# Rank 20 products for one block of units or for two at once, in a retention block with a maxout FFN

## The chip, the cores and the metric

The kernel runs on one core of one Trainium2 chip. The metric is the device time of a run in microseconds (us), the median over several runs. The profile is one further execution of the same program, recorded instruction by instruction.

The engines appear under their short names in the profile: PE is TensorE (matmuls; PEld are its weight loads), DVE is VectorE, ACT is ScalarE, POOL is GpSimd, SP is the engine that issues most of the transfers. TensorE writes its sums to PSUM[...].

## The reference

The first half is retention in parallel form, over 8 batches, 8 heads, 576 positions, head size 64; the second is a feed-forward network with a maximum of three products:

```
scores = scale * q @ k.T
ret    = scores * Dmat            # gamma_h ** (i - j) for i >= j, else 0
x      = (ret @ v)  as (B*S, H*D) # 4608 tokens x 512
h      = max(x @ w1, x @ w2, x @ w3)   # 4608 x 768
out    = h @ w_out                # 4608 x 512
```

Everything is fp32 here; the weights come as float64 and are converted on the chip.

## The kernel before, in words

**Tiles and stages.** The tokens are cut into 9 tiles of 512 (`t` = 0 to 8), each of four chunks of 128. While the feed-forward network of tile `t` runs, the retention of tile `t + 1` is woven into it. The last loop does this: `steps(t + 1)` gives twelve lists of retention steps, and after each list the generator `ffn(t)` is advanced by one part. The engines take their instructions in program order, so this loop, together with two lists of small deferred steps, sets the order. `soon` appends VectorE work of the retention to `urgent`; `chore` pops one step from `urgent` (or from `chores`, which holds sums of weights); `scale` pops one multiplication of keys by their decay on ScalarE. Inside the products these pops are made at fixed step numbers (lines 785 to 793).

**Retention.** Chunks 0 to 7 go through transposed keys and queries (`transposes`), masked scores (`scores`, tiles `st`), states (`state`, `keep`) and outputs (`values`). From chunk 8 on it is done in halves of 64 positions: `chunk_scores` writes masked scores into the tiles `m0` and `m1` (the latter holds the transposed queries first) and keeps the running state stacked with the values in `va`; `chunk_values` multiplies the two. VectorE transposes, masks, adds the states and scales the output into `xT`; GpSimd multiplies the state in `va` by the decay `gs_of` (line 335).

**The up products.** `h` of a tile has 6 blocks of 128 units (`fb`), taken in pairs (`fp`). Tile 0, and pair 1 of tile 1, are computed plainly (`up_plain`). All others use a scheme in which 20 products stand for the 24 that a block needs for 512 tokens: each multiplies a combination of weight blocks (`w_sb`, `n`, summed once by `weight_sums`) with a combination of quarters of `x` (`s`, summed per tile by `sums_of_x`), 256 tokens wide. `PRODUCTS` gives their order:

```
PRODUCTS = """E a11 b12, E a14 b42, B s15 n5, A a22 b21, C s3 b23, B s19 b41, A s10 b32, C a13 b31, B s6 n2, A s13 b22,
              C a11 b11, B s14 n1, A s11 n4, D s7 b43, B a23 n6, A s20 b33, D s16 b13, B a21 n3, A a21 n8, A a24 n7"""
```

The letters are five chains of sums in PSUM, which differ in where they end. A and B take turns in the two banks of `ps_x`; E, C and D take turns in the two banks of `ps_y`, so D uses E's bank and the next E uses C's. A product is named by its chain and its number there: A3 is the third on chain A. After most products the running sum of the chain is copied by ScalarE to SBUF into a `part` (line 698), and the chain goes on adding in the same bank. `JOINS` lists what VectorE then adds, or takes the maximum of, to turn parts into the two halves of `h` (line 693): 14 copies and 14 joins per block. Two of the joins read a chain's bank directly: B1's reads E, C3's reads C. The last nine joins of a block follow D2 (three), B6 (three) and A7 (three); B6's first one gives the low half of `h` (tokens 0 to 255), A7's last one gives the high half.

`up` does this for one block `fb`: 20 products, one at a time, with banks half used (256 of 512 values). In tile 1 the blocks come in the order 2, 3, 0, 1, 4, 5, in later tiles 0, 1, 4, 5, 2, 3.

**The down products.** `downs` multiplies `h` with `w_out` by seven products of half-size blocks, in the order 1, 2, 6, 7, 5, 4, 3; each runs over all three pairs `fp` and both halves of 128 tokens, 12 matmul instructions. Product 1 reads the low half of `h` for the even block of every pair, product 2 for the odd block; 6, 7, 5 and 3 read sums of `h` that `sums_of_hidden` makes on VectorE and GpSimd. `kept` copies a product's bank to parts, `total` adds it to another product and stores.

**Buffers.** `ppool` holds the parts, 20 slots of 1 KB under the tag `part`; the decay table `gs` and the states of the first eight chunks are in the same ring. `att` holds `kT` (2 buffers), `m0` and `m1` (3 each).

Of the kernel before, what the change touches and what calls it, by code (L numbers as in the profile page):

```python
# [53 lines left out]
AHEAD = 3  # L54
FILL = 192
PARTS = 20

# [24 lines left out]
def kernel(  # L82
# [184 lines left out]
    def transposes(g):  # L267
        both = qks[g] = {}
        if g >= BY_CHUNKS:
            for n, tag in (("k", "kT"), ("q", "m1")):  # L270
                both[n] = att.tile([P, H, D], FP32, tag=tag, name=tag, bufs=2 if n == "k" else 3)
            ms[g, 0], ms[g, 1] = att.tile([P, H, D], FP32, tag="m0", name="m0"), both["q"]
        else:
            for n in ("k", "q"):
                tag, bufs = ("kT", 2) if n == "k" else (f"m{g % 2}", 3)
                both[n] = att.tile([P, NP, C], FP32, tag=tag, name=n + "T", bufs=bufs)
        if g >= BY_PE:
            for n in ("k", "q"):
                soon(partial(nc.vector.transpose, both[n][:].rearrange("a p c -> a (p c)"),
                             raws.pop(("kx" if n == "k" else n, g))[:].rearrange("a x y i -> a (x y i)")))  # L280
            return
        for n, src in (("k", raws["k", g]), ("q", raws.pop(("q", g)))):
            pool, tag = (ps_r, "r") if g >= CPT else (ps_x, "x")
            pt = pool.tile([P, NP, C], FP32, tag=tag, name=n + "t")
            for p in range(NP):
                nc.tensor.transpose(pt[:, p, :], pair(src, p), ident[:C, :C])
            nc.scalar.copy(both[n][:], pt[:])

    def scores(g):
        chore(len(urgent))  # L290
        scale(len(scaling))
        if g >= BY_CHUNKS:
            chunk_scores(g)
            return
        qT, kT = qks[g]["q"], qks[g]["k"]
        s = [ps_r.tile([C, NP, C], FP32, tag="r", name=f"s{j}") for j in range(2)]
        for p in range(NP):
            for j in range(2):
                r = slice(D * j, D * (j + 1))
                nc.tensor.matmul(s[j][:, p, :], lhsT=kT[r, p, :], rhs=qT[r, p, :], start=True, stop=True)  # L300
        for j in range(2):
            st = sts[g, j] = att.tile([C, NP, C], FP32, tag=f"m{j}", name="st")
            soon(partial(nc.vector.tensor_tensor, st[:], s[j][:],
                         masks[start_of(g)][:].unsqueeze(1).to_broadcast([C, NP, C]), op=ALU.mult))
# [44 lines left out]
    def state_factors():  # L349
        for j in range(2):  # L350
            nc.scalar.copy(gs_of[half(1), j::2].unsqueeze(2), gs[half(j), :, 0:1])

# [15 lines left out]

    def keep(g):
        def step(t, kv):  # L370
            if start_of(g) is not None:
                nc.vector.tensor_tensor(t[:], kv[:], gs[:], op=ALU.mult)
            else:
                nc.vector.tensor_tensor(t[:], kv[:], states[g][:], op=ALU.add)
                nc.gpsimd.tensor_tensor(t[:], t[:], gs[:], op=ALU.mult)
# [156 lines left out]
    def downs(t, h):  # L532
# [4 lines left out]
        def summed(n):  # L537
# [6 lines left out]
              5: summed(1), 6: summed(2), 7: summed(3)}  # L544

        def bank(pool, tag, name):
            b = pool.tile([P, NM, DM // 2], FP32, tag=tag, name=name)
            return [(m, whole, b[:, m, :]) for m in range(NM)]

# [52 lines left out]
        for group in ([[piece] for piece in x] if last else [x]):  # L602
            product(3, group, False)
            for m, cols, o in group:
# [78 lines left out]

    def up(t, h, fb):

        lo, hi = h[:, fb, 0:NH], h[:, fb, NH:NT]
        ps, of = {}, {}  # L690

        def join(out, a, b, op=ALU.add):
            nc.vector.tensor_tensor(out, a, b, op=op)  # L693

        def after(step):
            if step not in ("E1", "E2", "C2", "C3", "A6", "B5"):
                t = of[step] = ppool.tile([P, NH], FP32, tag="part", name="part")
                nc.scalar.copy(t[:], ps[step[0]][:])  # L698
            for out, ins, op in JOINS.get(step, ()):
                ins = [ps[n[0]] if n in ("E", "C") else of[n] for n in ins]  # L700
                join({"lo": lo, "hi": hi}.get(out) if out in ("lo", "hi") else of[out][:],
                     *(x[:] for x in ins), op)

        done = {}
        for chain, x, w in PRODUCTS:
            n = done[chain] = done.get(chain, 0) + 1
            if n == 1:
                pool, tag = (ps_x, "x") if chain in "AB" else (ps_y, "y")
                ps[chain] = pool.tile([P, NH], FP32, tag=tag, name=chain.lower())
# [3 lines left out]
            nc.tensor.matmul(ps[chain][:], lhsT=factor(w, fb), rhs=xS[t][x], start=n == 1, stop=ends,  # L713
                             skip_group_check=True)
            after(f"{chain}{n}")
            yield

# [25 lines left out]
    def ffn(t):  # L743
# [28 lines left out]
        if t == 1:  # L772
            spread.append(True)
            weight_sums(0)
            weight_sums(2)
        plain = (2, 3) if t == 1 else ()
        order = (2, 3, 0, 1, 4, 5) if t == 1 else (0, 1, 4, 5, 2, 3)
        total = sum(24 if fb in plain else len(PRODUCTS) for fb in order)
        count = parts = 0
        for n, fb in enumerate(order):  # L780
            if fb not in plain:
                while fb // 2 not in summed_fp:
                    chore()
            steps_of_one = up_plain_all(t, h, fb) if fb in plain else up(t, h, fb)
            for step, cost in enumerate(steps_of_one):
                if fb in plain:
                    chore(4 if (fb, step) == (plain[-1], 1) else 8)
                elif step % 4 == 1 or step % 4 == 3 and len(urgent) > 6:
# [9 lines left out]
            if n % 2:  # L798
                sums_of_hidden(h, fb // 2)
                if fb in plain:  # L800
                    weight_sums(fb // 2)
        chore(len(urgent))
# [6 lines left out]

    def up_plain_all(t, h, fb):  # L810
        for i in range(3):
            up_plain(t, h, fb, i)()
            yield 8
# [146 lines left out]
```

## Time and profile before

| | |
|---|---|
| time, median of three runs | 764.6 us (763.73 to 766.52) |
| the profiled run | 763.31 us, span of its trace 761.3 us |
| TensorE busy | 749.7 us (98%), 5928 matmul instructions |
| VectorE busy | 594.4 us (78%) |
| ScalarE busy | 385.6 us (51%) |
| GpSimd busy | 91.5 us (12%) |
| joins (line 693), part to part | 460 at a mean of 470 ns |
| copies of chains (line 698) a and b | 276 at 369 ns, 230 at 372 ns |
| granted TensorE clock | full throughout |

A row of instruction groups in the profile reads: line, engine, operation, names of what is written and read, shape, count, then busy time and the mean of one in ns, then the idle time of the engine just before these instructions and which instruction ended most of it. In a row of waits the engine, name and line before the arrow waited for the one behind it; then follow the total in us, the number of times and the longest. In the timeline each row is a start, a length, an engine and an instruction, with the number merged into the row.

One fp32 matmul of the program is two matmul instructions on TensorE, so 920 products appear as 1840.

### The profile page before, as it was taken

What the parts mean: (1) busy time and instruction counts of PE and PEld (TensorE: products, weight loads), DVE (VectorE), ACT (ScalarE), POOL (GpSimd) and SP (SyncE); (2) the same over time, 40 slices, a digit from 0 to 9 for tenths busy, and PEclk for the clock granted to TensorE, in tenths of its full rate; (3) what the DMA queues carried; (4) which work ended last, traced back from release to release, by engine and by line L of the source; (5) the groups of instructions that cost most, each with busy time, mean ns of one, the idle gap of its engine ahead of it and who ended that gap; (6) DMA issues with size and microseconds to landing.
All of it is one profiled execution on the core that took longest, in us unless ns stands there. A gap on an engine that the chain in (4) does not pass through costs nothing.

```text
span 761.3 us, 16127 instructions
## 1 busy us (share of the span) xinstructions
PE 749.7 (98%) x5928; PEld 604.7 (79%) x5928; DVE 594.4 (78%) x1274; ACT 385.6 (51%) x1051; POOL 91.5 (12%) x112
## 2 busy tenths in 40 slices
PE   8999999999999999999999999999999999999998
PEld 7645444688878888888888888888888888888887
DVE  2998998979888967797788859885889677955771
ACT  3664641365256635664466446643665266515551
POOL 3210122102010111011011102010102011100000
PEclk9999999999999999999999999999999999999999
DMA  9995753404241514242333324242414141000001
GB/s 222 242 240 130 200 108 80 87 9 84 80 81 34 91 45 96 45 74 54 81 74 58 68 69 87 37 79 65 90 29 94 45 91 33 2 29 28 1 1 56
DMA packets 230318, 59.39 MB, mean 78 GB/s; under 512 B 211168, under 2 KB 228960, under 8 KB 230240
## 3 DMA queue, kind: packets, MB, share of 16 engines
q1 hardware_dynamic: 229664, 58.04, 35.2%
q8 instruction: 46, 0.75, 0.4%
q10 hardware_dynamic: 576, 0.33, 0.1%
q14 instruction: 32, 0.26, 0.1%
HBM read 48.89 MB, written 9.44 MB: 77 GB/s over the span
## 4 chain that ended last, share of the span: by engine, by line
PE 86%; DVE 9%; SPq 2%; DMA 1%; issue 1%; ACT 0%; DVEq 0%; ACTq 0%
PE a L713 15%; PE b L713 13%; PE dx L553 11%; PE up L736 11%; PE c L713 6%; PE dz L553 5%; PE d L713 5%; PE e L713 4%; DVE part L693 4%; PE o L436 4%; PE down L723 3%; PE dy L553 3%; DVE m L325 2%; PE sk L317 2%; SPq L218 1%; DMA qraw<-in_q_dram 1%
## 5 line engine op out<-in xcount | busy, mean ns | idle before, releaser
L693 DVE TENSOR_TENSOR part<-part 128x256 f32<-128x256 f32 x460 | 211.7, 470 | 62.4 <-ACT part L698 53.9
L698 ACT COPY part<-a 128x256 f32<-128x256 f32 x276 | 101.8, 369 | 65.8 <-PE a L713 60.3
L698 ACT COPY part<-b 128x256 f32<-128x256 f32 x230 | 85.6, 372 | 94.3 <-PE b L713 88.3
L736 PE MATMUL up<-xT,w 128*128 128x512 f32 (+2 forms) x200 | 84.7, 579 | 1.6 <-DVE w L642 1.6
L713 PE MATMUL a<-s,w 128*128 128x256 f32 x276 | 82.2, 380 | 0.0
L713 PE MATMUL b<-s,n 128*128 128x256 f32 x276 | 82.1, 379 | 0.0
L736 PEld LDWEIGHTS up<-xT,w 128*128 128x128 f32 x200 | 36.8, 190 | 43.6 <-issue 38.4
L186 ACT ACTIVATE kraw<-kraw,gk 128x64 f32<-128x64 f32 x208 | 66.9, 349 | 0.7 <-DMA kraw<-in_k_dram 0.4
L713 PE MATMUL d<-s,w 128*128 128x256 f32 x184 | 56.3, 388 | 2.8 <-DVE part L693 2.6
L335 POOL TENSOR_TENSOR va<-va,gs_of 64x512 f32<-64x512 f32 x24 | 26.9, 1120 | 263.9 <-DVE va L333 157.8
L713 PEld LDWEIGHTS b<-s,n 128*128 128x128 f32 x276 | 52.5, 190 | 7.1
L713 PEld LDWEIGHTS a<-s,w 128*128 128x128 f32 x276 | 51.5, 190 | 8.1 <-ACT part L698 0.2
L713 PE MATMUL b<-xT,n 128*128 128x256 f32 x184 | 56.6, 389 | 0.0
L713 PE MATMUL c<-xT,w 128*128 128x256 f32 x184 | 54.9, 380 | 0.0
L713 PE MATMUL e<-xT,w 128*128 128x256 f32 x184 | 47.3, 380 | 0.7 <-DVE part L693 0.7
L713 PE MATMUL a<-xT,n 128*128 128x256 f32 x184 | 47.2, 379 | 0.0
L325 DVE TENSOR_TENSOR m<-sk,gm 64x512 f32<-64x512 f32 x56 | 38.5, 688 | 8.4 <-PE sk L321 7.2
L553 PE MATMUL dx<-To,H 128*128 128x256 f32 (+1 forms) x204 | 44.9, 371 | 0.0
L693 DVE TENSOR_TENSOR h<-part 128x256 f32<-128x256 f32 x92 | 39.1, 425 | 6.9
L713 PEld LDWEIGHTS d<-s,w 128*128 128x128 f32 x184 | 33.7, 190 | 12.7 <-DVE part L693 8.7
L560 ACT COPY part<-dx 128x256 f32<-128x256 f32 (+1 forms) x34 | 10.5, 362 | 63.4 <-PE dx L553 56.7
L553 PEld LDWEIGHTS dx<-To,H 128*128 128x128 f32 x204 | 36.6, 190 | 4.8
(121 smaller groups left out, 1351.9 us busy)
## 6 DMA issues: line engine op xcount, KB each, us to landing
bits<-in_moe_w_dram SPq DMA_DIRECT2D x36, 256.0 KB, 4.9
out_dram<-osb SPq DMA_DIRECT2D x35, 256.0 KB, 2.1
kraw<-in_k_dram SPq DMA_DIRECT2D x32, 256.0 KB, 3.1
qraw<-in_q_dram SPq DMA_DIRECT2D x224, 32.0 KB, 2.1
kxraw<-in_k_dram SPq DMA_DIRECT2D x224, 32.0 KB, 2.1
va<-in_v_dram SPq DMA_DIRECT2D x56, 128.0 KB, 3.1
bits<-in_moe_w_out_dram SPq DMA_DIRECT2D x6, 512.0 KB, 6.4
vraw<-in_v_dram SPq DMA_DIRECT2D x7, 256.0 KB, 4.6
```

What stands on the lines that cost most here:

```text
L186: scaling.popleft()()
L317: nc.tensor.matmul(sk[c][half(c), h, :], lhsT=kr[half(c), h, :], rhs=vas[g, c][half(c), h, :], start=True, stop=True)
L325: nc.vector.tensor_tensor(ms[g, c][half(c)], sk[1 - c][half(c)], gm[half(c)], op=ALU.mult)
L335: nc.gpsimd.tensor_tensor(to[half(1)], to[half(1)], gs_of[half(1)].unsqueeze(2).to_broadcast([D, H, D]), op=ALU.mult)
L436: nc.tensor.matmul(o[half(c), n % 2, n // 2, half(m)], lhsT=vas[g, m][:, h, :], rhs=ms[g, m][:, h, :], start=m == 0 and n == 0, stop=True, ...
L553: nc.tensor.matmul(o, lhsT=hS[n](fp)[:, m * P:(m + 1) * P], rhs=late["T"][n][:, fp, cols], start=first and fp == 0 and (m == 0 or last and ...
L560: nc.scalar.copy(both[m][:, cols], o)
L693: nc.vector.tensor_tensor(out, a, b, op=op)
L698: nc.scalar.copy(t[:], ps[step[0]][:])
L713: nc.tensor.matmul(ps[chain][:], lhsT=factor(w, fb), rhs=xS[t][x], start=n == 1, stop=ends, skip_group_check=True)
L723: nc.tensor.matmul(b[:], lhsT=h[:, fb, m * P:(m + 1) * P], rhs=w_sb["out", fb], start=(fb == 0), stop=(fb == NF - 1))
L736: nc.tensor.matmul(ps[:, cols], lhsT=w_sb[i, fb][:, dc * P:(dc + 1) * P], rhs=xT[t][:, dc, cols], start=dc == 0 and cols.start == 0, stop= ...
```

## The change

`up` takes a pair of blocks, `fp`, in place of one block. Each of the 20 products is issued for block `2 * fp` and then for `2 * fp + 1`, into the two halves of one PSUM bank; the flag that starts a bank's sums is set on the first of the two alone. Copies and joins follow the second and are 512 wide. The parts that end up as the two halves of `h`, A1 and A2, are copied into `h` at once and joined there, so a pair takes 12 slots of `ppool` where two blocks took 28. The ring has 11 slots, now of 2 KB.

Around it: `kept`, `total` and the last copy of `downs` treat a bank in one instruction. `gs` becomes a constant of 4 values per partition that is broadcast where it is used, and its load fetches 4 bytes per row and head pair in place of 256. The transposed queries of chunks 0 to 7 move from `m0`/`m1` to the ring of parts. `m0` has two buffers, taken in `chunk_scores` and no longer in `transposes`. The order of the pairs is that of the blocks before, and the steps that pop deferred work keep their numbers, counted over 40 steps of a pair and no longer twice over 20. `FILL`, an unused tile, has 160 bytes for 192.

```diff
-FILL = 192
-PARTS = 20
+FILL = 160
+PARTS = 11
...
-         "B6": [("lo", ("A2", "A3"), ALU.max), ("A5", ("A5", "B4"), ALU.add), ("A5", ("A5", "D1"), ALU.add)],
-         "A7": [("A1", ("A1", "B6"), ALU.add), ("A1", ("A1", "A5"), ALU.max), ("hi", ("A1", "A7"), ALU.max)]}
+         "B6": [("A2", ("A2", "A3"), ALU.max), ("A5", ("A5", "B4"), ALU.add), ("A5", ("A5", "D1"), ALU.add)],
+         "A7": [("A1", ("A1", "B6"), ALU.add), ("A1", ("A1", "A5"), ALU.max), ("A1", ("A1", "A7"), ALU.max)]}
...
+    gs = const.tile([P, NP], FP32, name="gs")
-    gs = ppool.tile([P, NP, D], FP32, tag="part", name="gs")
...
-            ms[g, 0], ms[g, 1] = att.tile([P, H, D], FP32, tag="m0", name="m0"), both["q"]
+            ms[g, 1] = both["q"]
         else:
-            for n in ("k", "q"):
-                tag, bufs = ("kT", 2) if n == "k" else (f"m{g % 2}", 3)
-                both[n] = att.tile([P, NP, C], FP32, tag=tag, name=n + "T", bufs=bufs)
+            both["k"] = att.tile([P, NP, C], FP32, tag="kT", name="kT", bufs=2)
+            both["q"] = ppool.tile([P, NP, C], FP32, tag="part", name="qT")
...
-            st = sts[g, j] = att.tile([C, NP, C], FP32, tag=f"m{j}", name="st")
+            st = sts[g, j] = att.tile([C, NP, C], FP32, tag=f"m{j}", name="st", bufs=2 + j)
...
+        ms[g, 0] = att.tile([P, H, D], FP32, tag="m0", name="m0", bufs=2)
         nc.scalar.copy(ms[g, 0][half(1)], ms[g, 1][half(1)])
...
         def kept(src):
-            both = [ppool.tile([P, NH], FP32, tag="part", name="part") for _ in range(NM)]
-            for m, cols, o in src:
-                nc.scalar.copy(both[m][:, cols], o)
+            both = ppool.tile([P, NM, NH], FP32, tag="part", name="part")
+            for m, cols, o in together(src):
+                nc.scalar.copy(both[:, m, cols], o)
...
-            for m, cols, o in src:
-                nc.vector.tensor_tensor(osb[:, m, cols], o, others[m][:, cols], op=ALU.add)
+            for m, cols, o in together(src):
+                nc.vector.tensor_tensor(osb[:, m, cols], o, others[:, m, cols], op=ALU.add)
...
-    def up(t, h, fb):
+    def up(t, h, fp):
+        two = slice(2 * fp, 2 * fp + 2)
+        ps, of = {}, {"A1": h[:, two, NH:NT], "A2": h[:, two, 0:NH]}
...
             if step not in ("E1", "E2", "C2", "C3", "A6", "B5"):
-                t = of[step] = ppool.tile([P, NH], FP32, tag="part", name="part")
-                nc.scalar.copy(t[:], ps[step[0]][:])
+                if step not in of:
+                    of[step] = ppool.tile([P, 2, NH], FP32, tag="part", name="part")[:]
+                nc.scalar.copy(of[step], ps[step[0]][:])
...
-            nc.tensor.matmul(ps[chain][:], lhsT=factor(w, fb), rhs=xS[t][x], start=n == 1, stop=ends,
-                             skip_group_check=True)
-            after(f"{chain}{n}")
-            yield
+            for e in range(2):
+                nc.tensor.matmul(ps[chain][:, e, :], lhsT=factor(w, 2 * fp + e), rhs=xS[t][x],
+                                 start=n == 1 and e == 0, stop=ends, skip_group_check=True)
+                if e == 1:
+                    after(f"{chain}{n}")
+                yield
...
-                nc.sync.dma_start(gs[half(j)], state_decay[half(j), :, half(j)])
+                nc.sync.dma_start(gs[half(j)].unsqueeze(2), state_decay[half(j), :, D * j:D * j + 1])
```

More of the change, by code (lines that the diff above doesn't have):

```diff
@@ L350, in state_factors @@
         for j in range(2):
-            nc.scalar.copy(gs_of[half(1), j::2].unsqueeze(2), gs[half(j), :, 0:1])
+            nc.scalar.copy(gs_of[half(1), j::2], gs[half(j)])
     def key_masks():
@@ L369, in keep @@
     def keep(g):
+        factor = gs[:].unsqueeze(2).to_broadcast([P, NP, D])
         def step(t, kv):
             if start_of(g) is not None:
-                nc.vector.tensor_tensor(t[:], kv[:], gs[:], op=ALU.mult)
+                nc.vector.tensor_tensor(t[:], kv[:], factor, op=ALU.mult)
             else:
                 nc.vector.tensor_tensor(t[:], kv[:], states[g][:], op=ALU.add)
-                nc.gpsimd.tensor_tensor(t[:], t[:], gs[:], op=ALU.mult)
+                nc.gpsimd.tensor_tensor(t[:], t[:], factor, op=ALU.mult)
         if begins(g):
@@ L544, in downs, with together @@
               5: summed(1), 6: summed(2), 7: summed(3)}
+        banks = {}
         def bank(pool, tag, name):
             b = pool.tile([P, NM, DM // 2], FP32, tag=tag, name=name)
-            return [(m, whole, b[:, m, :]) for m in range(NM)]
+            pieces = [(m, whole, b[:, m, :]) for m in range(NM)]
+            banks[id(pieces)] = [(whole, whole, b[:])]
+            return pieces
+        def together(src):
+            return banks.get(id(src), src)
         def product(n, out, first):
@@ L603, in downs @@
             product(3, group, False)
-            for m, cols, o in group:
+            for m, cols, o in together(group):
                 nc.scalar.copy(osb[:, m, cols], o)
@@ L682, in convert @@
             next(converting, None)
-    def up(t, h, fb):
[L689 to L693, printed above, removed]
+    def up(t, h, fp):
+        two = slice(2 * fp, 2 * fp + 2)
+        ps, of = {}, {"A1": h[:, two, NH:NT], "A2": h[:, two, 0:NH]}
         def after(step):
             if step not in ("E1", "E2", "C2", "C3", "A6", "B5"):
-                t = of[step] = ppool.tile([P, NH], FP32, tag="part", name="part")
[L698 to L702, printed above, removed]
+                if step not in of:
+                    of[step] = ppool.tile([P, 2, NH], FP32, tag="part", name="part")[:]
+                nc.scalar.copy(of[step], ps[step[0]][:])
+            for dst, ins, op in JOINS.get(step, ()):
+                a, b = (ps[n][:] if n in ("E", "C") else of[n] for n in ins)
+                nc.vector.tensor_tensor(of[dst], a, b, op=op)
         done = {}
@@ L708, in up @@
                 pool, tag = (ps_x, "x") if chain in "AB" else (ps_y, "y")
-                ps[chain] = pool.tile([P, NH], FP32, tag=tag, name=chain.lower())
+                ps[chain] = pool.tile([P, 2, NH], FP32, tag=tag, name=chain.lower())
             while x not in made[t]:
@@ L775, in ffn @@
             weight_sums(2)
-        plain = (2, 3) if t == 1 else ()
-        order = (2, 3, 0, 1, 4, 5) if t == 1 else (0, 1, 4, 5, 2, 3)
-        total = sum(24 if fb in plain else len(PRODUCTS) for fb in order)
+        plain = 1 if t == 1 else None
+        order = (1, 0, 2) if t == 1 else (0, 2, 1)
+        total = sum(48 if fp == plain else 2 * len(PRODUCTS) for fp in order)
         count = parts = 0
-        for n, fb in enumerate(order):
-            if fb not in plain:
-                while fb // 2 not in summed_fp:
+        for fp in order:
+            if fp != plain:
+                while fp not in summed_fp:
                     chore()
[L784 to L787, printed above, removed]
+            for step, cost in enumerate(up_plain_all(t, h, fp) if fp == plain else up(t, h, fp)):
+                if fp == plain:
+                    chore(4 if step == 4 else 8)
                 elif step % 4 == 1 or step % 4 == 3 and len(urgent) > 6:
@@ L797, in ffn @@
                     yield
[L798 to L801, printed above, removed]
+            sums_of_hidden(h, fp)
+            if fp == plain:
+                weight_sums(fp)
         chore(len(urgent))
@@ L808, in ffn, with up_plain_all @@
         yield
[L810 to L813, printed above, removed]
+    def up_plain_all(t, h, fp):
+        for fb in (2 * fp, 2 * fp + 1):
+            for i in range(3):
+                up_plain(t, h, fb, i)()
+                yield 8
     warm(6)
```

## The prediction

> **What bounds the kernel now.** I read the page's busy table first, then the chain that ended last, then the waits of the weight loads and matmuls, then the timeline around one such wait, then the groups by shape.
>
> ```profile
> PE 749.7 (98%) x5928; PEld 604.7 (79%) x5928; DVE 594.4 (78%) x1274; ACT 385.6 (51%) x1051; POOL 91.5 (12%) x112
> ...
> PE 86%; DVE 9%; SPq 2%; DMA 1%; issue 1%; ACT 0%; DVEq 0%; ACTq 0%
> ```
>
> TensorE is the bound: 98% busy, 86% of the chain. No other engine is near full, so shorter work on VectorE or ScalarE pays only where TensorE stands still for it. Those places are in the weight-load waits (waiter, released by: us in total, times, longest):
>
> ```profile
> PEld d L713 <- DVE part L693: 8.7, 15, 1.4
> ...
> PEld a L713 <- ACT part L698: 3.0, 13, 0.6
> ...
> PEld e L713 <- DVE part L693: 1.1, 1, 1.1
> ```
>
> One of the fifteen, on TensorE and then on VectorE (start, length, instruction, count, idle before it):
>
> ```profile
> 303.23 0.60 PE L713 MATMUL b<-s,n 128*128 128x256 f32 x2
> 303.66 0.66 PE L713 MATMUL a<-s,n 128*128 128x256 f32 x2
> 304.59 0.70 PE L713 MATMUL d<-s,w 128*128 128x256 f32 x2 [0.27 <-DVE part L693]
> 305.12 0.59 PE L713 MATMUL b<-xT,n 128*128 128x256 f32 x2
> ...
> 303.38 0.69 DVE L325 TENSOR_TENSOR m<-sk,gm 64x512 f32<-64x512 f32 x1
> 304.11 0.42 DVE L693 TENSOR_TENSOR part<-e,part 128x256 f32<-128x256 f32 x1
> ```
>
> A product (two matmul instructions) starts every 0.43 us: 303.23, 303.66, and the next should be 304.09. Chain d needs the bank of chain e, which the join of B1 has to read first. That join belongs to the third product, but VectorE is late and runs it at 304.11, after which d starts at 304.59. Lost: 0.50, and 0.10 more, since the next product follows after 0.53. So the idle figure beside the matmul (0.27) understates it.
>
> All such losses: a weight load normally starts 0.21 ahead of its matmul, so 15 waits of 8.7 in total moved the d matmuls by 8.7 - 15 x 0.21 = 5.5 us, plus 15 x 0.10 = 1.5 for the restart: 7.0. Chain e once, at 227.66 instead of 226.78, plus 0.10: 1.0. Of the thirteen a-waits all but one are the usual lead; the long one cost about 0.4. **At most 8.4 us (1.1% of the span) is there to win in the products.**
>
> [...] The trace has 369 to 372 and 571 to 588[...]. [...]
>
> ```profile
> 216.30 1.23 POOL L335 TENSOR_TENSOR va<-va,gs_of 64x512 f32<-64x512 f32 x1 [24.56 <-DVE va L333]
> ...
> 216.54 2.19 DVE L693 TENSOR_TENSOR part<-part 128x256 f32<-128x256 f32 x3
> ...
> 307.02 1.34 DVE L693 TENSOR_TENSOR part<-part 128x256 f32<-128x256 f32 x3 [0.32 <-ACT part L698]
> ```
>
> Three joins take 2.19 beside GpSimd and 1.34 without it: 0.85 dearer. [...]
>
> **The change, part by part.**
>
> ```profile
> L693 DVE TENSOR_TENSOR part<-part 128x256 f32<-128x256 f32 x460 | 211.7, 470 | 62.4 <-ACT part L698 53.9
> L693 DVE TENSOR_TENSOR h<-part 128x256 f32<-128x256 f32 x92 | 39.1, 425 | 6.9
> ...
> L740 DVE TENSOR_TENSOR h<-h,up 128x512 f32<-128x512 f32 x16 | 10.9, 682 | 2.3 <-PE up L736 2.2
> ...
> L741 ACT COPY h<-up 128x512 f32<-128x512 f32 x8 | 4.6, 571 | 10.7 <-PE up L736 10.7
> ```
>
> *Matmuls.* 46 units become 23 pairs with the same 920 products, weight loads and shapes. Nothing is gained on TensorE itself.
>
> *Joins.* 644 (14 per unit) become 322 of double width. A 512-wide operation takes 682 to 732 ns (w<-mant,expo, both inputs in SBUF, 732). From the x3 line a dependent 256-wide join costs 0.447, 0.03 over a lone 0.42, so I take 0.71 for a dependent 512-wide one. Busy time goes from 289 us (with the e and c joins' 38) to 322 x 0.71 = 229. VectorE gains 60 us, all of it beside TensorE, so none of it counts directly.
>
> *Copies.* 644 x 0.37 become 322 x 0.58: 51 us less on ScalarE, also beside TensorE.
>
> *The d and e waits.* D1 is product 13, counted from 0. Before it, VectorE has the previous unit's nine last joins (9 x 0.45 = 4.0 us) plus attention work, against 13 x 0.43 = 5.6 us. In a pair the nine joins take 9 x 0.71 = 6.4 us against 26 x 0.43 = 11.2 us. Margin 4.8 us instead of 1.6, and at most two attention transposes (0.70 each) are queued ahead of the e join. Those waits go. In a chain, the copy (0.04 + 0.58) lies under four steps of 0.43, 1.73 us, where before 0.37 lay under 0.86. So the a wait goes too: minus 8.4.
>
> *The new wait, at the start of the down products.* Product 1 reads the low half of h for even blocks, product 2 for odd. Before, the even block of the last pair was finished a unit earlier. Now both are finished together, by the first join of B6, behind the three of D2. From the end of D2's slot: 0.16 matmul drain, 0.04 to ScalarE, 0.08 for a key scaling ahead of the copy, 0.58 copy, 0.03 to VectorE, 4 x 0.71 joins, 0.06 to TensorE, 0.10 restart = 3.9 us. TensorE gets there after B6, A6 and A7 for two blocks each (six steps of 0.43) and the two steps that read block pair 0: 8 x 0.43 = 3.45. So it stands 0.45 us in tiles 2 to 8 (order of pairs 0, 2, 1). In tile 1 pair 2 is last and is read two matmuls later: nothing. 7 x 0.45 = **plus 3.1**. Bounds: 0 (shorter joins) to 1.3 per tile (a GpSimd scaling beside the joins adds 0.85).
>
> *Score matmuls of the third pair* need the second chunk's transposes, which stand behind the previous pair's nine joins: ready about 6.8 us after the pair's start, needed at 14 x 0.43 + 1.0 = 7.0. That is thin: 0 to 0.6 a tile, I take 0.07: **plus 0.5**.
>
> *h as destination, eleven 2 KB slots.* A1 and A2 are copied into h 3.5 us or more after the last down product read the old h, so ScalarE doesn't wait. A pair takes twelve slots of eleven: slot twelve and the next pair's first fall on parts last read in A3's and D2's joins. The latter end about 2.5 us before the next B1 copy. Nothing.
>
> *kept, total and the last copy of downs.* 512 wide: each delays its reader by about 0.2 us, hidden behind the 2.59 us of the product between.
>
> *qT in the parts' pool, m0 with two buffers taken at the scores.* The scores of a pair follow the values of the pair before, so two suffice; ScalarE's copy into m0 is queued at the same place as before. *FILL* moves addresses only. Nothing for either.
>
> *gs.* 128 KB in 512 packets becomes 2 KB in 512 packets; SP issues two DMAs as before, ahead of later key and value loads. At the 222 GB/s of the first slice 128 KB is 0.6 us, and the first stage waits on loads; packets of 4 bytes aren't free. 0 to 0.6, taken as **minus 0.3**.
>
> Sum: -8.4 + 3.1 + 0.5 - 0.3 = **-5.1 us** on a span of 761.3. That profiled run took 763.31, below the three timed runs' median of 764.6 (763.73 to 766.52), so I put the change on the median: **759.5 us**, 0.7% faster. About 0.5% (3.8 us) is what a measurement of this kernel can tell from no change.
>
> **Rivals.** *Full gain (0.15):* the joins run nearer 0.68 and the products' start is hardly held; only the -8.4 and -0.3 and some 0.5 remain: 756.4. For it: L740's 682. Against it: a dependent chain of four.
> *Hidden anyway (0.15):* VectorE runs in program order, so the e join stays behind masks and transposes and d still waits as often; the new wait eats the rest: 763 to 765. For it: in the example the 0.69 mask was directly ahead of the e join. Against: the margin above.
> *Slower (0.20):* VectorE at the end of a pair becomes the bound. GpSimd's scaling of va (1.12 us), which I expect to end 0.2 us before D2's joins, falls on them: the new wait is 1.3 us, and in the third pair another such overlap turns the thin score margin into 0.55. 7 x 1.85 = 13, less 8.4 and 0.3: about 769. It decides from 1.2 us per tile on (8.4 / 7). For it: joins of 0.73 at 216.54. Against: in the last tile there is no attention, and the overlap needs both places.
>
> **How the numbers follow.** My forecast has 0.50, of which 0.45 is below 760.8 and 0.05 above. Full gain 0.15 is faster; hidden 0.15 is the same; slower 0.20 splits 0.18 and 0.02. Faster 0.60, same 0.22, slower 0.18. The forecast's own range is 757.5 to 761.5; for 8 in 10 it reaches from the full gain with its unknowns (755.5) into the slower case (768).
>
> **What would show it.** Joins: 322, near 0.70. Weight loads of d waiting on a join: gone, from 8.7 us to under 1. A new wait of dx on the h join, seven times, 0.3 to 0.7 us each. Score matmuls waiting on a transpose: under 1 us in all. TensorE's count unchanged. Wrong if dx waits over 1.2 us per tile, if d waits persist, or if the first 25 us stretch.

## The result and the profile after

The changed kernel takes 757.27 us (median of 4 runs, 757.02 to 758.12), the kernel before 764.16 us beside it (4 runs, 763.57 to 766.52): ratio 0.9906, 95% interval 0.9883 to 0.9929. Faster by 0.9%, and 2.2 us below the forecast of 759.5: just below its own range (757.5 to 761.5) and inside that for 8 in 10 (755.5 to 768). The profiled run took 757.02 us, its span is 755.2 us against 761.3 before.

First the busy table of the page after, and the engines' shares of its chain:

```profile
PE 747.1 (99%) x5928; PEld 608.1 (81%) x5928; DVE 535.6 (71%) x929; ACT 342.6 (45%) x700; POOL 91.3 (12%) x112
...
PE 92%; DVE 4%; DMA 2%; ACT 2%; SPq 1%; issue 0%; POOL 0%; DVEq 0%; ACTq 0%; POOLq 0%
```

The 5928 matmuls stay. VectorE lost 58.8 us of work and ScalarE 43.0, in 345 and 351 fewer instructions. None of that appears in the time by itself: VectorE's share of the chain fell from 9% to 4% because TensorE waits for it less. The waits of the weight loads on VectorE or ScalarE that concern the change (waiter, released by: us in total, times, longest):

```profile
PEld dx L562 <- DVE h L708: 3.5, 7, 0.5
...
PEld sk L321 <- DVE m L191: 1.1, 1, 1.1
...
PEld d L720 <- ACT part L705: 0.4, 1, 0.4
```

The fifteen waits of chain d on a join (8.7 us) and that of chain e (1.1) are gone. New are seven of the first down product, `dx`, on the join that completes the low half of `h`, as forecast, one of score matmuls on a transpose, in tile 1, and one of chain d on a copy just behind it. The groups by shape (line, engine, operation, count, busy, mean ns, idle before):

```profile
L708 DVE TENSOR_TENSOR part<-part 128x512 f32<-128x512 f32 x161 | 111.3, 691 | 94.2 <-ACT part L705 91.8
L708 DVE TENSOR_TENSOR h<-h,part 128x512 f32<-128x512 f32 x115 | 79.7, 693 | 28.2 <-ACT h L705 24.2
...
L705 ACT COPY part<-b 128x512 f32<-128x512 f32 x115 | 67.4, 586 | 140.4 <-PE b L720 140.4
```

A join of 512 takes 0.69 us (0.71 forecast) and a copy 0.586 (0.58, from copies of 512 at 571 to 588 ns in the trace before). Both engines now mostly wait for TensorE, or for each other, as their idle columns say: of the 94.2 us of idle time before the joins of parts, 91.8 ended with a copy, and the copies of `b` waited 140.4 us for TensorE.

The new wait, in the timeline at the end of a tile (start, length, instruction, count, idle before it):

```profile
341.14 1.04 POOL L335 TENSOR_TENSOR va<-va,gs_of 64x512 f32<-64x512 f32 x1 [4.74 <-PE a L720]
...
342.33 2.14 DVE L708 TENSOR_TENSOR part<-part 128x512 f32<-128x512 f32 x3 [1.32 <-ACT part L705]
...
344.10 3.15 PE L562 MATMUL dx<-w_out,h 128*128 128x256 f32 x12
344.51 0.69 DVE L708 TENSOR_TENSOR h<-h,part 128x512 f32<-128x512 f32 x1
...
345.25 1.59 PEld L562 LDWEIGHTS dx<-w_out,h 128*128 128x128 f32 x8 [0.53 <-DVE h L708]
```

After its first four `dx` matmuls TensorE needs the pair just finished. Its weight load stands until the `h` join ends at 345.20, behind the three joins of D2. The twelve take 3.15 us where twelve that do not wait take 2.75 (the forecast had 0.45 a tile; this is 0.40). GpSimd's scaling of `va` ended at 342.18, 0.15 us before D2's joins.

Where the time went, from the starts of the first `dx` matmul of each tile in the two timelines. The third row is the later run e1, in which no `dx` waits: a floor for this program.

| us | to the first `dx` of tile 1 | from each to the next, tiles 1 to 8 | sum of the seven |
|---|---|---|---|
| before | 185.56 | 81.72, 79.90, 79.62, 79.75, 80.23, 80.50, 72.34 | 554.06 |
| after | 186.11 | 78.80, 79.19, 79.19, 79.22, 79.19, 79.19, 72.54 | 547.32 |
| e1 | 186.22 | 78.80, 78.80, 78.79, 78.79, 78.80, 78.80, 72.15 | 544.93 |

Before stood 9.1 us above the floor between these marks, after 2.4. That is 6.7 us gained; up to the first mark 0.55 was lost. From the last mark to the end of the span both take 21.7 us. Tile 8's `dx` wait of 0.4 is in the second, but from the start of the last matmul to the end it needs 3.16 us where before needed 3.53. Together these are the 6.1 by which the spans differ.

### The profile page after: what moved, and what is told of

Its sections match the earlier page's. It is cut to its first block, busy times and chain, and to the rows that moved or that the text cites. A ratio compares the mean times of both kernels' runs of the same rounds, so it can differ in the third digit from the quotient of the medians.

```text
span 755.2 us, 15101 instructions
## 1 busy us (share of the span) xinstructions
PE 747.1 (99%) x5928; PEld 608.1 (81%) x5928; DVE 535.6 (71%) x929; ACT 342.6 (45%) x700; POOL 91.3 (12%) x112
## 4 chain that ended last, share of the span: by engine, by line
PE 92%; DVE 4%; DMA 2%; ACT 2%; SPq 1%; issue 0%; POOL 0%; DVEq 0%; ACTq 0%; POOLq 0%
PE a L720 17%; PE b L720 15%; PE dx L562 11%; PE up L744 10%; PE c L720 8%; PE dz L562 5%; PE e L720 5%; PE d L720 5%; PE o L438 4%; PE down L731 3%; PE sk L317 3%; PE dy L562 3%; DVE part L708 2%; ACT part L705 1%; DMA vraw<-in_v_dram 1%; PE sk L321 1%
## 5 line engine op out<-in xcount | busy, mean ns | idle before, releaser
L708 DVE TENSOR_TENSOR part<-part 128x512 f32<-128x512 f32 x161 | 111.3, 691 | 94.2 <-ACT part L705 91.8
L705 ACT COPY part<-b 128x512 f32<-128x512 f32 x115 | 67.4, 586 | 140.4 <-PE b L720 140.4
L708 DVE TENSOR_TENSOR h<-h,part 128x512 f32<-128x512 f32 x115 | 79.7, 693 | 28.2 <-ACT h L705 24.2
L705 ACT COPY part<-a 128x512 f32<-128x512 f32 x92 | 53.9, 586 | 48.5 <-PE a L720 48.1
L720 PE MATMUL a<-s,w 128*128 128x256 f32 x276 | 70.9, 379 | 0.0
L720 PE MATMUL b<-s,n 128*128 128x256 f32 x276 | 70.8, 379 | 0.0
L532 POOL TENSOR_TENSOR H<-h 128x256 f32<-128x256 f32 x24 | 20.2, 842 | 285.6 <-DVE h L708 285.6
L720 PE MATMUL d<-s,w 128*128 128x256 f32 x184 | 47.3, 380 | 0.0
L720 PE MATMUL b<-xT,n 128*128 128x256 f32 x184 | 47.2, 379 | 0.0
L720 PEld LDWEIGHTS e<-xT,w 128*128 128x128 f32 x184 | 35.0, 190 | 5.2 <-DVE va L331 0.2
```

What stands on the lines that cost most here:

```text
L532: urgent.append(lambda: (pool(s3, a11, a21, op=ALU.subtract), pool(s4, a12, s2, op=ALU.subtract)))
L705: nc.scalar.copy(of[step], ps[step[0]][:])
L708: nc.vector.tensor_tensor(of[dst], a, b, op=op)
L720: nc.tensor.matmul(ps[chain][:, e, :], lhsT=factor(w, 2 * fp + e), rhs=xS[t][x], start=n == 1 and e == 0, stop=ends, skip_group_check=True)
```

## The experiments

Each is an edit to the kernel after, or to an earlier experiment where its text says so; e3 edits the kernel before. Lines left out of an edit are marked by `...` or described. Times are medians, with the range of the runs; ratios are to the kernel before, run on the same chip.

**e1, the last pair last.** The down products take the pair that was finished last as their third, so the first read of it comes four matmuls later.

```diff
+        pairs = (1, 0, 2) if t == 1 else (0, 2, 1)
-            for fp in range(NF // 2):
+            for n_fp, fp in enumerate(pairs):
...
```

> The changed kernel, but every down product takes the pair that was finished last as its last one (order 0, 2, 1 in tiles 2 to 8, and 1, 0, 2 in tile 1), so the first read of the late half of h comes two matmul steps of 0.43 us later. Theory (the wait of dx on the h join is a plain race between a chain of four joins and the matmuls before the read; it costs 0.29 us plus 0.10 of restart in each of seven tiles): 0.86 us covers 0.39, the seven waits of dx on h vanish and the time falls by 2.7 us against the changed kernel, to about 754.5. Rival (the wait only moves, since products 6 and 7 hang on the same joins through the sums of h): dx and dz wait on H instead and the time stays within 0.8 us of 757.3.

754.78 us (754.5 to 755.12), ratio 0.9884, interval 0.987 to 0.9897. At the same place in the timeline:

```profile
343.82 2.75 PE L563 MATMUL dx<-w_out,h 128*128 128x256 f32 x12
344.23 0.69 DVE L709 TENSOR_TENSOR h<-h,part 128x512 f32<-128x512 f32 x1
```

The `h` join still runs 0.4 us after `dx` began, but now its reader is four matmuls further on. `dx` takes 2.75, and the intervals are flat at 78.80. The new wait cost 2.5 us in the time, for 7 x 0.40 = 2.8 in the timeline.

**e2, wide copies with narrow joins.** Every join is issued as two of 256.

```diff
-                nc.vector.tensor_tensor(of[dst], a, b, op=op)
+                for e in range(2):
+                    nc.vector.tensor_tensor(of[dst][:, e], a[:, e], b[:, e], op=op)
```

> The changed kernel, with every join of a pair issued as two joins of 256, block by block, so 644 joins again; matmuls, copies and order stay. Theory (the gain came from the distance between a join and the matmul that needs its bank, not from fewer VectorE instructions): no wait of d on a join comes back. The low half for the even block is then the seventh of eight short joins; neighbours that don't depend on each other start every 0.34 us in the trace of before, so it is ready after 6 x 0.34 + 0.42 = 2.5 us where four joins of 512 took 2.9, and the wait of dx shrinks from 0.29 to about 0: 0 to 2.7 us less than the changed kernel, 754.6 to 757.3. Rival (fewer and larger VectorE instructions are what made it faster): VectorE's busy time goes back towards 594 us, d or sk waits return and the time rises by 3 us or more, to 760 or above.

755.03 us (754.79 to 756.82), ratio 0.9893, interval 0.9878 to 0.9908.

```profile
PE 745.2 (99%) x5928; PEld 608.3 (81%) x5928; DVE 550.1 (73%) x1251; ACT 342.0 (45%) x700; POOL 90.3 (12%) x112
...
342.26 2.10 DVE L709 TENSOR_TENSOR part<-part 128x256 f32<-128x256 f32 x6 [1.25 <-ACT part L705]
...
344.04 2.75 PE L562 MATMUL dx<-w_out,h 128*128 128x256 f32 x12
344.28 0.75 DVE L709 TENSOR_TENSOR h<-h,part 128x256 f32<-128x256 f32 x2
```

No wait of chain d on a join came back, at 644 narrow joins and more work on VectorE than in after. So it is not fewer or wider joins that removed these waits. What this run keeps of the change is the wide copies and the 26 products, in place of 13, ahead of a pair's first on chain d; no run parts these two. Here too `dx` runs through. Product 1 reads only the even block, whose 256-wide join is the first of the two. Its first part ends 0.66 us after `dx` began, where the wide join ended at 1.10. Of the 0.44 between them 0.27 is the shorter join and the rest its earlier start, so most of the loss was the granularity of that one join; the run does not part it from the three narrow joins ahead. With its joins broken up, on a VectorE that is busy for 73% of the span, the run is 2.2 us faster than after (755.03 for 757.27). The 322 additional instructions cost almost nothing: six of 256 take 2.10 us together, three of 512 took 2.14, so two neighbours that do not depend on each other start 0.34 us apart ((2.10 - 0.42) / 5), though one alone is recorded as 0.42.

**e3, the d wait undone in the kernel before.** ScalarE copies E2 as well, and the join of B1 reads the copy. Chain d then no longer needs a join to free its bank.

```diff
-JOINS = {"B1": [("B1", ("E", "B1"), ALU.add)], ...
+JOINS = {"B1": [("B1", ("E2", "B1"), ALU.add)], ...
...
-            if step not in ("E1", "E2", "C2", "C3", "A6", "B5"):
+            if step not in ("E1", "C2", "C3", "A6", "B5"):
```

> The kernel before, one block at a time, with one edit: ScalarE also copies chain E after its second product, and B1's join reads that part and no longer the bank. So the d matmul needs only ScalarE to have left E's bank; ScalarE gets 46 copies more (17 us busy), VectorE keeps its 644 joins. Theory (7.0 us of the gain are waits of d on the late e join): weight loads of d waiting on a join go from 8.7 us to under 1, and the time falls by 6 to 7 us against the kernel before, to about 757.5, with no change in width anywhere. Rival (the width is what counts: less work on VectorE and ScalarE): the time stays within 2 us of 764, or the wait passes to another matmul that ScalarE or VectorE is late for.

758.89 us (758.26 to 760.42), ratio 0.9941, interval 0.9928 to 0.9953: 4.6 us gained, less than expected. No d wait is left, but a join wait of chain e grew:

```profile
PEld e L713 <- DVE part L693: 3.4, 4, 2.4
```

Chain e shares its bank with C, which a join also frees. Its one long wait, in tile 2, moved the matmuls by 2.2 us against 0.9 before, and a score matmul stood 1.3 us against 0.5. Adding these 2.1 us to the gain gives 6.7, about the 7.0 of the d waits. So those waits were real and recoverable without wide joins; the wide joins also removed the e wait, which the copy alone did not.

**e4 and e4_again, the full decay table.** The kernel after, with `gs` loaded as the table of 128 KB in the ring again.

```diff
-    gs = const.tile([P, NP], FP32, name="gs")
+    gs = ppool.tile([P, NP, D], FP32, tag="part", name="gs")
...
-                nc.sync.dma_start(gs[half(j)].unsqueeze(2), state_decay[half(j), :, D * j:D * j + 1])
+                nc.sync.dma_start(gs[half(j)], state_decay[half(j), :, half(j)])
```

> The changed kernel with gs as it was: the full table of 256 values per partition in the ring of parts, loaded with 128 KB, and read without a broadcast. A look at the first stage alone. Theory (the 0.6 us by which the first up product starts earlier, 24.36 against 24.96, come from 126 KB less ahead of the later loads): the first up product starts at 24.8 to 25.1. Rival (they come from elsewhere, the queries' new place or the layout): it stays at 24.2 to 24.5.

> The kernel with the full gs table once more, unchanged. Its one look had a first up product that began at about 29.8 us, 5.5 us after the changed kernel's, with the first three slices moving 193 to 209 GB/s where the changed kernel had 221 to 242. If the 126 KB or the table's place cause this, every run is near 763. If it was one bad start of the loads, the timed runs lie at 757.3 plus at most 1, and the new profile's first up product starts between 24.3 and 26.

763.91 us in a single run, and 763.74 us (761.76 to 767.06) in the repeat with 20 runs, ratio 0.999, interval 0.998 to 1.0001. Nearly the whole gain was gone, against every expectation of the first run. The intervals between the `dx` starts were those of the kernel after (79.19), but the first came at 192.56 and 196.08 us for 186.11. The loss lay at the start, where the loads are. The edit had done a second thing: without the small `gs` every later tile of SBUF moved. No trace prints an address. The small `gs` has 16 bytes per partition; if it takes up 32, which is my assumption, the move is 32 bytes, and the change's `FILL` of 160 for 192 exactly makes room for it, so before and after have these tiles at the same place. e8 below agrees: with `FILL` at 192 and no small `gs`, as in before, it takes 758.16 us.

**e8, the table with the tiles put back**, by `FILL = 192` on top of e4; and **e9, the shift alone**, `FILL = 128` in the kernel after.

> The kernel after with the full decay table of 128 KB in the ring again, as in e4, but with the unused tile at 192 bytes, so that every later tile of SBUF has the address offset that it has in the kernels before and after. Theory (e4's loss of 6 us came from the 32 bytes by which all later tiles had moved, not from the table): 757.3 to 758.2 us, first up product before 26.5 us in the profile. Rival (the table's 128 KB itself delays the start): about 763.5, first up product after 28 us.

> The kernel after with the unused tile at 128 bytes in place of 160, and nothing else changed: all later tiles of SBUF lie 32 bytes lower, the small decay table stays. Theory (the offset of 32 bytes slows the loads): about 763.5 us, first up product after 28 us. Rival (the offset does nothing, e4 was slow because of the table): 757.3, first up product at 24.4 to 25.9 us.

e8: 758.16 us (757.03 to 758.29), ratio 0.9913, interval 0.9884 to 0.9942. e9: 763.18 us (759.34 to 765.34, 20 runs), ratio 0.9982, interval 0.997 to 0.9995. So the shift does it and not the table, whose 0.9 us between the medians is not told from nothing. The first up product of e9 came at 26.83 us, not after 28 as expected; most of the loss came later than I had put it. The queue of the loads, and what the 16 DMA engines moved in each fortieth of the span, after and then e9 (queue: packets, MB, share of 16 engines' span):

```profile
q1 hardware_dynamic: 229664, 57.91, 35.3%
GB/s 228 221 242 136 209 109 78 91 4 81 73 91 46 102 32 96 45 78 51 81 74 69 59 61 95 51 62 67 92 31 93 43 95 33 1 30 28 1 1 56
```

```profile
q1 hardware_dynamic: 229664, 57.91, 38.5%
GB/s 193 204 209 157 164 173 97 86 21 68 66 103 46 79 48 84 70 69 58 66 88 62 65 57 97 29 85 60 81 43 97 43 89 38 1 22 36 1 1 55
```

The same packets and bytes took 10% more DMA time: 0.385 x 761.3 = 293 us for 0.353 x 755.2 = 267. In the first 60 us, where the DMA engines are full (shares of 0.94 and 0.99 in the two halves of it in after), 193 to 209 GB/s replaced 221 to 242, and the loads came late. The stretch from 30 to 60 us, after and then e9 (length; busy time of PE, PEld, DVE, ACT, POOL; clock, DMA share, GB/s; the share counts a packet where it starts and can pass 1):

```profile
30.00:60.00 30.00, 29.77 (x117) 14.43 (x116) 29.20 (x53) 20.80 (x33) 3.79 (x3) 1.00 0.99 228
```

```profile
30.00:60.00 30.00, 26.90 (x120) 13.72 (x119) 26.24 (x50) 19.86 (x31) 3.31 (x3) 1.00 1.13 211
```

TensorE was busy for 2.9 us less here and for 2.0 less in the 30 us before. By packet size, the mean time of a packet of 256 bytes rose from 18.2 to 20.7 ns and of one of 1024 from 56.5 to 66.2, but that of one of 128 only from 12.9 to 13.0. That is 14% more for the pieces of 256 bytes, 17% for those of 1024 and 1% for those of 128. Only this one offset was tried, so the runs show that it costs, but not by what mechanism, nor which other offsets would.

**e5, transposes queued earlier.** e1, and the transposes of a chunk are put on the list of deferred VectorE work one part earlier, to remove the score matmuls' wait in tile 1.

```diff
-            at(m, (transposes, b))
+            at(m - 1 if n else m, (transposes, b))
```

> The last pair last in the down products, and besides the transposes of every second chunk pair's later chunk moved one step earlier in the list, ahead of the third pair. Theory (in tile 1 the score matmuls stand 1.15 us for the transpose of queries that is queued behind the second pair's nine joins, and a d product 0.19 + 0.10 us after it): both go, 1.4 us less than with the order of pairs alone (754.8), so 753.4. Rival (VectorE is only asked earlier for the same work, and a join of the second pair comes late instead): no change within 0.7 us, and a wait of d or of dx on a join in tile 1.

755.35 us (753.85 to 756.02), ratio 0.9869, interval 0.9848 to 0.989: nothing gained over e1. The wait was untouched:

```profile
PEld sk L321 <- DVE m L191: 1.1, 1, 1.1
```

Work on that list is taken in turn, one entry in four steps while the list is short. An earlier entry behind the same others does not come out earlier: the two transposes start at 171.71 and 172.34 us here, at 171.60 and 172.22 in e1. In the timeline of the kernel after, tile 1:

```profile
168.50 2.17 DVE L708 TENSOR_TENSOR h<-h,part 128x512 f32<-128x512 f32 x3
170.59 0.69 DVE L708 TENSOR_TENSOR part<-e,part 128x512 f32<-128x512 f32 x1
171.19 0.70 DVE L191 STREAM_TRANSPOSE kT<-kxraw 128x512 f32<-128x512 f32 x1
171.82 0.67 DVE L191 STREAM_TRANSPOSE m<-qraw 128x512 f32<-128x512 f32 x1
...
172.54 0.27 PE L321 MATMUL sk<-m,kT 64*64 64x64 f32 x2 [0.94 <-DVE m L191]
```

**e11, the list emptied faster in tile 1.** e5, with the list popped at every second step in tile 1 when it holds two entries or more.

```diff
-                elif step % 4 == 1 or step % 4 == 3 and len(urgent) > 6:
+                elif step % 4 == 1 or step % 4 == 3 and len(urgent) > (1 if t == 1 else 6):
```

> e1 with the transposes queued one part earlier, as in e5, and in tile 1 the list of deferred VectorE work also popped at every second step when it holds two entries or more (in later tiles seven or more, as it was). Theory (what tile 1 lost is the transpose of the queries standing behind the second pair's nine joins): the score matmuls' wait of 1.15 us in tile 1 is gone, about 1.4 below e1, 753.4 us. Rival (the pops then put transposes ahead of joins that a chain or the down products need): a d, e or dx wait appears in tile 1 in its place, 754.8 or more.

753.36 us (752.86 to 755.68), ratio 0.9861, interval 0.9833 to 0.9889, the fastest of all medians here. The last transpose before those scores now comes at 168.65, ahead of the joins of A7, and its scores start at 170.97 without a wait on VectorE:

```profile
168.03 0.70 DVE L191 STREAM_TRANSPOSE kT<-kxraw 128x512 f32<-128x512 f32 x1
...
168.65 0.67 DVE L191 STREAM_TRANSPOSE m<-qraw 128x512 f32<-128x512 f32 x1
169.25 2.17 DVE L709 TENSOR_TENSOR h<-h,part 128x512 f32<-128x512 f32 x3
...
170.97 0.27 PE L321 MATMUL sk<-m,kT 64*64 64x64 f32 x2
```

VectorE ran the two transposes where the list now puts them, 3.6 us earlier than in e1 (168.03 for 171.60), and the joins after them. The first `dx` of tile 1 starts at 185.17, 1.05 us before e1's, and neither a d, e nor `dx` wait on a join appears in its place. So the order on VectorE was what tile 1 lost. The 1.4 us between the medians of e11 and e1 fit it, though their runs overlap.

**e6, more work on VectorE.** Four maxima of a value with itself in every pair, 92 in all, 63.5 us at 0.69 each; values unchanged. VectorE's busy time rose by 72.3 us, to 607.9.

```diff
                 nc.vector.tensor_tensor(of[dst], a, b, op=op)
+            if step in ("A2", "A3", "B4", "A4"):
+                nc.vector.tensor_tensor(of[step], of[step], of[step], op=ALU.max)
```

> The changed kernel with four more 512 wide operations of VectorE in every pair (after A2, A3, B4 and A4, the maximum of a part with itself, which leaves it as it is): 92 x 0.69 = 64 us more work, which brings VectorE's busy time from 536 back to 594 or more, as in the kernel before, at places where no matmul waits within several us. Theory (VectorE's busy time is worth nothing by itself): within 1.5 us of the changed kernel's 757.3, no d waits. Rival (the 60 us saved on VectorE are what the gain came from): 761 or more, with d or sk waits back.

765.79 us (764.73 to 768.67), ratio 1.0014, interval 1.0006 to 1.0023: 8.5 us lost, more than the whole change had won. My theory missed, and the rival's figure came by another way than it said: d stayed without a wait on a join, and `dx` waited longer.

```profile
PEld dx L562 <- DVE h L708: 11.4, 8, 2.2
...
346.09 1.41 DVE L333 TENSOR_TENSOR va<-sk,va 64x512 f32<-64x512 f32 x2
...
347.54 2.87 DVE L708 TENSOR_TENSOR part<-part 128x512 f32<-128x512 f32 x3
347.64 1.49 POOL L335 TENSOR_TENSOR va<-va,gs_of 64x512 f32<-64x512 f32 x1 [6.21 <-PE b L722]
...
351.19 1.99 PE L562 MATMUL dx<-w_out,h 128*128 128x256 f32 x8 [1.77 <-DVE h L708]
```

This is the forecast's slower rival in action. VectorE updates `va` late, so D2's joins begin only 0.86 us ahead of `dx` (1.77 in after), and GpSimd's scaling now falls on them: 2.87 us for 2.14. Together 0.91 + 0.73 = 1.6 us more wait in this tile, 1.9 in place of 0.3. The scaling falls on these joins in tiles 1 to 6, where `dx` waits 1.2 to 2.0 us; in tile 7 it waits 0.5 without it, and in tile 8, which has no scaling, 0.3 as in after. Both are longer here: the three joins by the 0.73 us, GpSimd's multiply at 1.49 us for 1.04.

**e10, the same load where it should be harmless.** The four maxima in all pairs but the last of each tile.

```diff
+            if fp != (2 if t == 1 else 1) and step in ("A2", "A3", "B4", "A4"):
...
```

> The four extra 512-wide maxima of a value with itself, after A2, A3, B4 and A4 as in e6, but only in the pairs that are not the last of their tile: 15 pairs x 4 x 0.69 = 41 us more work on VectorE, values unchanged. Theory (VectorE's load counts only where its last joins hold the down products, at the end of a tile's last pair): within 1.2 us of the kernel after, 757 to 758.5, first down product's wait at 0.3 in seven tiles as before. Rival (VectorE's load as such has become a limit, e6's 8.5 us spread over all pairs): 761.5 or more.

758.4 us (757.57 to 760.01), ratio 0.9924, interval 0.9898 to 0.995.

```profile
PE 746.8 (99%) x5928; PEld 607.7 (80%) x5928; DVE 580.3 (77%) x989; ACT 342.6 (45%) x700; POOL 94.6 (13%) x112
...
PEld dx L562 <- DVE h L708: 3.5, 7, 0.5
```

44.7 us more on VectorE, and the time moved by 1.1, which the runs' ranges cannot tell from nothing; the `dx` waits are those of after. Of e6's loss 7.4 us came with the eight last pairs, which held about a third of the added work.

**e7, one more join in the chain of D2**, a maximum of A3 with itself; values unchanged.

```diff
-         "D2": [..., ("A3", ("A3", "C1"), ALU.add)],
+         "D2": [..., ("A3", ("A3", "C1"), ALU.add), ("A3", ("A3", "A3"), ALU.max)],
```

> The changed kernel with one more 512 wide maximum (A3 with itself) at the end of D2's joins, so that five dependent joins in place of four stand ahead of the low half of h. Theory (the wait of dx is the end of this chain): each of the seven waits grows by 0.72 us from 0.29 to 1.0, and the time rises by 5.0 us, to about 762.3, back near the kernel before. Rival (the wait hangs on something else, such as ScalarE's copy or the semaphore): the time rises by under 2 us.

764.38 us (763.72 to 765.37), ratio 1.0002, interval 0.9992 to 1.0013: with one more operation of 0.69 us per pair the whole gain is gone.

```profile
PEld dx L562 <- DVE h L708: 9.0, 8, 1.3
```

The seven waits grew from 0.29 to 1.02 us beside the restart, by the operation's length and no slack, as expected: 7 x 0.73 = 5.1. The first `dx` of tile 1 came at 187.56, 1.45 us later than in after. Of that, 1.03 was there before the first pair that has the longer chain (its first product began at 146.61 for 145.58 us), so the edit does not explain it and its cause is open; in tile 1 the score wait went from 1.15 to 1.87 us, while the d wait of 0.3 was gone. From that first product to the last matmul the trace is 6.1 us longer than after's; with the 1.0 this is where 764.4 came from instead of 762.3.

## Why the prediction was right, step by step

Sign, mechanism and place were right; the gain was 6.9 us between medians and 6.1 between spans, for 5.1. Of the 2.2 us below 759.5, 0.4 come from the kernel before, at 764.16 for 764.6. The time is nearer to the full gain's 756.4 than to 759.5; what speaks for the forecast is the `dx` wait, which that rival all but denied and which stands in seven tiles. Between the spans the sum fell 1.0 short. It missed 1.4 of gain in the products, 0.3 at the `dx` wait and 0.3 at the two ends of the program; that it also missed a loss of 1.0 at the scores hid half of this, by luck.

- *Waits in the products, -8.4.* They went, as said. Summing how late each product's matmul started in the trace before gives d 6.7, e 1.0, a 0.5 and some 0.8 in delays of under 0.1 us, which the table of waits does not show: 9.0. Score matmuls gave another 0.8 that the sum left out. This term was 1.4 too small, because of these two small kinds. e3 shows the d part of it alone.
- *The new `dx` wait, +3.1.* Seven times, in tiles 2 to 8, and absent in tile 1, as forecast: 7 x 0.40 = 2.8. e1 and e2 take it away by two different edits (2.5 and 2.2 us), e7 lengthens it by what its chain is lengthened.
- *Scores behind joins, +0.5.* The mechanism was right and its spread wrong. The margin held in tiles 2 to 8 and failed once, in tile 1, by 1.15 us, just over the 1 us named as the sign; with a d wait of 0.3 after it, 1.5 against the 0.7 of d and a waits that tile 1 had before. e11 removes it.
- *`gs`, -0.3.* The measured terms above, -9.8, +2.8 and +1.5, leave 0.6 of the 6.1. In the traces 0.4 of it lies behind the last matmul, where the sum had no term and no run shows the cause, and 0.2 at the start: the first product of the scheme begins at 145.58 us for 145.77. In the seven other runs with after's loads (e1, e2, e5, e6, e7, e10, e11) this mark lies anywhere from 145.45 to 146.87, and e8, with the table, is 0.9 us above after in the median, with overlapping ranges. The term is not resolved. That small packets are not free holds: in the trace before a packet of 4 bytes took 9.3 ns on average, one of 256 bytes 18.2.
- *`FILL`, nothing.* Right in its figure and wrong in its reason. A move of 32 bytes costs 6 us, as e9 shows (763.18 for 757.27). By the count in e4, which e8 supports and no trace shows, it cost nothing because the small `gs` moves the later tiles back by as much.
- *The slower rival* (769, deciding from 1.2 us per tile) did not happen: GpSimd ended 0.15 us before D2's joins in the tile shown (0.2 forecast). That was close: in tiles 2 to 5 the distance is 0.05 to 0.15. e6 shows the rival happening, with 1.9 us in the tile shown and 765.8 in all, so its mechanism is real. The score waits in the third pair that it also counted were no part of it.
- *Hidden anyway* fell with the d waits; *full gain* (756.4) is what e1 and e2 reach and pass.

Better than both kernels is e11, 753.36 us; its most certain part, e1, gives 754.78.

## What to carry to other kernels

Where TensorE is at 98%, price a wider VectorE or ScalarE instruction by the last dependent chain before a stage, not by busy time: 44.7 us more VectorE work in the wrong pairs cost nothing that could be measured, and one 0.69 us operation in each pair's last chain cost about 6. Let the stage read what was finished last in its last turn (2.5 us in e1). When an edit changes the size of any early SBUF tile, check the addresses of the tiles that take DMA loads before attributing the difference to the edit: 32 bytes were 6 us in e9.

## What the runs showed of the hardware

- A move of 32 bytes of the tiles that take the loads: 10% more DMA time for the same packets, 193 to 209 GB/s in place of 221 to 242, and 6 us of 757.
- Independent neighbours on VectorE overlap: 256-wide joins 0.34 us apart with 0.42 each; splitting every wide join in two added 14.5 us of busy time, not the 322 x (2 x 0.42 - 0.69) = 48 that the single durations suggest.
- A GpSimd multiply beside three 512-wide joins lengthens both: the joins from 2.14 to 2.87 us, and the multiply from 1.04 to 1.49 (e6 against after).
